# Moving five weight casts, one weight combination and five DRAM additions of x inside a fused attention, mixer and MLP kernel

## The chip, the core and the metric

The kernel runs on one core of a Trainium2 chip. The metric is the device time of one execution in microseconds (us), lower being better. TensorE (PE) does the matmuls and its separate weight loads (PEld), ScalarE (ACT) copies, casts and gelus, VectorE (DVE) additions and the attention arithmetic, GpSimd (POOL) a few small operations and all DMAs that add to their destination, and SyncE (SP) issues the plain DMAs.

## The reference, cut to what matters

With x of 2048 tokens by 576 channels and LN a layer norm without weights:

```python
xn = LN(x)
attn = sliding_window(xn @ wqkv, 32 heads of 18, 8 keys two tokens apart) @ wo
h    = shift_tokens(gelu(LN(xn) @ w1))          # by +1, -1, +2, -2 in four channel quarters
x1   = xn + h @ w2
mlp  = gelu(LN(x1) @ w3) @ w4                   # hidden size 4608
out  = x + attn + (x1 + mlp)
```

All data are float32. Each product is taken with both operands split into a float32r part and a rest, so that three (or, in the part below, seven) matmuls with chunks of the inner dimension stand where one would do.

## The kernel before, in words

The order of work on each engine is the order in which the program emits it, and the program is written out by hand. There are five stages: the qkv projection, the token mixer, four plain chunks of the MLP (the "units", 2 blocks of 128 hidden rows each), 28 groups of the MLP by a seven-product scheme, and the output projection of the attention with the final sums.

**The groups.** The scheme treats a pair of 128-row weight blocks and a pair of 512-token blocks as a 2x2 product and gets it with seven smaller products instead of eight, each of seven matmuls of 512 columns (function product, L1120 to L1133, matmul in L1130). They are called P1 to P7. Weights of group q lie in a tile WA[q] (w3a in the profile: A11, A22, A12) and a tile WS[q] (w3s: S1 to S4, sums and differences of blocks). The right-hand operands lie in five areas (x1n and xt in the profile). The loop over q (L1195) runs 28 times; q 0 to 13 (NWP = 14) work on tokens 0 to 1023, that is token tiles 0 to 7, and q 14 to 27 on tiles 8 to 15.

Between the products stand D0 to D7, the second MLP product of the group before it: each is one token tile (down, L859 to L881), 12 matmuls of 288 columns (L868), into one of two PSUM buffers. D0 to D3 take the tiles s0+4 to s0+7 and read the hidden halves c12 and c22, D4 to D7 the tiles s0 to s0+3 and read c11 and c21. After a tile's matmuls ACT empties the PSUM buffer, and then the buffer after next can be begun, seeded by ACT with the tile's running sum if that lies in SBUF. For the ten tiles in YD = (1, 2, 3, 5, 7, 9, 10, 11, 13, 15) the running sum lies in DRAM instead: ACT copies the PSUM buffer to one of a few staging tiles (L873) and POOL issues a DMA that adds it to yd[t] in DRAM (L874).

The order of a group is a string of item names; group 0 has an order of its own, in which only four tiles D0 to D3 stand, those of the last plain unit:

```python
ORDER = "P1 D0 P2 P6 D1 P5 D2 P7 D3 P4 D4 P3 D5 D6 D7"
ORDERS = {0: "P1 P2 D0 P6 P5 P7 D1 D2 P4 D3 P3", ...}
```

Products collect in PSUM, and ACT and DVE put them together: after P2 the first gelu (c11), after P6 and P7 a copy of the running bank by ACT ("keep", L1136), which the next product into that bank must wait for, and after P7 and P3 an addition by DVE (z_add, L1140). The addition behind P3 is the last one of the group; the gelus of c12 (L820, L821) follow it, and then low_part (L826), which takes the rest of the split. D0 of the next group is the first to read c12 and c22.

**The plan.** Everything else is hung on these items by at(item, function, arguments): it is emitted right behind the item, in the order of the at calls. What matters here:

- The next group's weights. load_pair (SP, L954 and L957) loads raw w3 blocks into the single tile w3st; split_a casts three blocks to WA (ACT L970 and L972, DVE L976) and lets POOL add a remainder from DRAM to its tail (L983); combine (L960 to L966) forms four sums and differences in w3st in place on DVE (L965, four instructions); split_s casts the result to WS and lets POOL add the tail (L992). In group 0 combine stood behind P4, ahead of D3 and P3, and low_part of c12 between the two halves of split_s.
- The output weight. In the last group (z = -1) five loads of wo rows go into tiles wr (SP, L1166 and L206) at the top of the loop body, and five split_wo follow (ACT cast L200, DVE subtraction L201), hung on D1, P5, D2, P7 and D4. Wo is first read by the output projection (L215), behind the last group's own eight D tiles.
- The residual x. load_xa(t) (L884 to L890) for a tile in YD lets POOL add x's tile to yd[t] by a DMA from DRAM to DRAM (L886). It was hung on D7 of groups 1 to 10, one tile of YD after the other.
- sums (L898 to L907): partial sums of the second half's operands, in DRAM, on D6 of groups 1 to 8; every other one is an adding DMA on POOL (L907).
- Attention runs on DVE in between: bg (L781) emits a few of its instructions behind every item until it is done.

**The end.** Behind the loop the last group's eight D tiles run back to back, with split_x of the attention's output blocks (ACT L181, L182, L187; DVE L183, L188) in between, then 16 token tiles of the output projection, 28 matmuls each (L215; the last tile L1437), with three PSUM buffers. DVE adds each to Y (L1431), for which load_y (SP, L1392) has brought the YD tiles back from DRAM. read_xo (SP, L174) loads the attention's output blocks; block 2 is loaded behind load_y of tiles 1, 2, 3 and 5.

Of the kernel before, what the change touches and what calls it, by code (L numbers as in the profile page):

```python
# [33 lines left out]
YD = (1, 2, 3, 5, 7, 9, 10, 11, 13, 15)  # L34
# [3 lines left out]
NWP = NF // 2 - NPL  # L38
# [19 lines left out]
def fused_block(ctx, tc, x, wqkv, wo, w1, w2, w3, w4, out):  # L58
# [448 lines left out]
    for b in range(NB):  # L507
        for i, m in enumerate((0, 1, 2, 4, 3) if b < 3 else (4, 0, 1, 2, 3)):
# [12 lines left out]
            k = {(0, 4): 0, (1, 1): 1, (1, 4): 2, (2, 1): 3, (2, 4): 4}.get((b, i))  # L521
# [102 lines left out]
    for t in range(NT):  # L624
# [19 lines left out]
        if t in (4, 5):  # L644
            r0, c0, n = ((256, 128, 128), (HF + 256, 0, 256))[t - 4]
# [8 lines left out]
        if t in (9, 10, 13, 14):  # L654
            k = {9: 4, 10: 6, 13: 8, 14: 10}[t]
# [168 lines left out]
    def low_part(h, g):  # L824
        spent[0] += 0.69
        dve.tensor_tensor(h[:, 1, :], g, h[:, 0, :].bitcast(F32), op=ALU.subtract)  # L826
# [182 lines left out]
    for u, (c, b) in enumerate(units):  # L1009
# [77 lines left out]
        k = u % 4  # L1087
# [107 lines left out]
    for q in range(NQ):  # L1195
        sb = q // NWP
# [28 lines left out]
        low12 = lambda: low_part(hid[q, "c12"], Z2)  # L1225
        n = q + 1
        plan = {}

        def at(it, f, *args):
            plan.setdefault(it, []).append(lambda: f(*args))  # L1230

        if q == 0:
            at("P6", split_op, 0, "T4")
            at("D1", gelu22)
            at("P7", split_a, n, (0, 1))
            at("D1", split_op, 0, "B22")
            at("D1", split_a, n, (2,))
            at("D2", low22)
            at("P4", combine, n)
            at("P3", gelu12)  # L1240
            at("P3", split_s, n, (0, 1))
            at("P3", low12)
            at("P3", split_s, n, (2,))
            at("P3", load_pair, q + 2)
        elif q == NWP - 1:
            rtemps[:] = [2, 13]
            at("P1", load_w4, p, 1)
            for it, k in zip(("P1", "P2", "P6", "P5", "P7", "P4", "P3"),
                             ("B11", "B21", "T2", "T1", "T3", "T4", "B22")):
                at(it, get_op, 1, k)  # L1250
            at("P4", split_w4, p)
            at("P3", split_op, 1, "B11", 0)
            at("D2", split_op, 1, "B11", 1)
            at("D3", gelu22)
            at("D4", low22)
            at("D4", split_op, 1, "B21", 0)
            at("D5", gelu12)
            at("D5", split_op, 1, "B21", 1)
            at("D6", low12)
            at("D6", split_op, 1, "T2", 0)  # L1260
            at("D7", split_op, 1, "T2", 1)
        elif q == NWP:
            rtemps[:] = [2]
            at("D0", split_op, 1, "T1", 0)
            at("D1", split_op, 1, "T1", 1)
            at("P1", split_op, 1, "T3", 0)
            at("D2", split_op, 1, "T3", 1)
            at("P2", split_op, 1, "T4", 0)
            at("P6", split_op, 1, "T4", 1)
            at("D3", split_op, 1, "B22", 0)  # L1270
            at("P5", split_op, 1, "B22", 1)
            at("P5", split_a, n, (0, 1))
            at("P7", split_a, n, (2,))
            at("P7", combine, n)
            at("D4", gelu22)
            at("P4", low22)
            at("D5", gelu12)
            at("D5", split_s, n, (0, 1))
            at("D6", low12)
            at("D6", split_s, n, (2,))  # L1280
            at("D7", load_pair, q + 2)
        elif z < -1:
            at("P1", load_w4, p, 1)
            at("P5" if q < NWP else "D2", split_a, n, (0, 1))
            at("D2" if q < NWP else "P7", split_a, n, (2,))
            at("D3", combine, n)
            at("P4", gelu22)
            at("D4", split_w4, p, 0)
            at("D4", low22)
            at("D5", split_w4, p, 1)  # L1290
            at("P3", split_s, n, (0, 1))
            at("D5", gelu12)
            at("D5", split_s, n, (2,))
            at("D6", low12)
            if z < -2:
                at("D6", load_pair, q + 2 + (q == NWP - 2))
        else:
            at("D3", split_w4, p)
            at("P4", gelu22)
            at("D4", low22)  # L1300
            at("D5", gelu12)
            at("D6", low12)
            for k, it in enumerate(("D1", "P5", "D2", "P7", "D4")):
                at(it, split_wo, k)
        if -5 <= z <= -2:
            for i, (it, nx) in enumerate((("P6", "D1"), ("P7", "D3"), ("P3", "D5"), ("D6", "D7"))):
# [6 lines left out]
            at("D5" if q else "P3", load_w4, NPL + pair(q + 1), 0)  # L1313
        if 0 < q < 9:
            at("D6", sums, 1, q - 1)
        if 0 < q <= len(YD):
            at("D7", load_xa, YD[q - 1])
        if -4 <= z < -1:
            at("P1", put_o, z + 4)
        if z == -2:  # L1320
# [149 lines left out]
```

## Time and profile before

| | before |
|---|---|
| median of three runs | 1298.65 us |
| lowest and highest | 1294.39, 1298.89 us |
| the profiled execution | 1297.69 us |
| its span in the trace | 1295.9 us |
| granted clock, mean | 0.993 |
| PE, DVE, ACT, POOL busy | 97%, 71%, 57%, 20% |
| DMA | 226.83 MB, mean 175 GB/s |

The span starts with the first instruction and ends with the last; the execution's own time is 1.79 us longer, for what lies around it. All times in the trace count from the span's start. A row of the timeline has the start, the duration, the engine (SPq is SP's sequencer, which issues DMAs), the line of the kernel, the operation and its tiles, and, in brackets, how long the engine had been idle before it and whose end released it. Rows merge neighbouring instructions of one kind (x7, x12). Matmuls are pipelined: from start to start, seven matmuls of a product take less than the duration of their row.

### The profile page before, as it was taken

What the parts mean: (1) busy time and instruction counts of PE and PEld (TensorE: products, weight loads), DVE (VectorE), ACT (ScalarE), POOL (GpSimd) and SP (SyncE); (2) the same over time, 40 slices, a digit from 0 to 9 for tenths busy, and PEclk for the clock granted to TensorE, in tenths of its full rate; (3) what the DMA queues carried; (4) which work ended last, traced back from release to release, by engine and by line L of the source; (5) the groups of instructions that cost most, each with busy time, mean ns of one, the idle gap of its engine ahead of it and who ended that gap; (6) DMA issues with size and microseconds to landing.
All of it is one profiled execution on the core that took longest, in us unless ns stands there. A gap on an engine that the chain in (4) does not pass through costs nothing. (4 is left out here: it accounts for less than half of the span.)

```text
span 1295.9 us, 20029 instructions
## 1 busy us (share of the span) xinstructions
PE 1262.2 (97%) x7482; PEld 1155.0 (89%) x7482; DVE 919.7 (71%) x1233; ACT 741.2 (57%) x1181; POOL 258.9 (20%) x374
## 2 busy tenths in 40 slices
PE   9999999999999999899999999998999999999798
PEld 8999998899899998799889988987899899899798
DVE  6456534778458978579989998988999983554342
ACT  3322226526545546677667776856876776776630
POOL 2011100021121212123222332211222222222100
PEclk9999999999999999999999999999999999999899
DMA  7646874256888987588888898696787769899872
GB/s 210 157 112 143 171 169 144 72 164 172 209 215 196 213 182 195 103 198 169 207 197 183 214 184 207 115 276 132 153 176 169 129 121 189 174 215 228 209 248 83
DMA packets 205565, 226.83 MB, mean 175 GB/s; under 512 B 79884, under 2 KB 140652, under 8 KB 205340
## 3 DMA queue, kind: packets, MB, share of 16 engines
q1 hardware_dynamic: 172332, 158.29, 43.0%
q0 software_dynamic: 33136, 67.26, 32.5%
q8 instruction: 59, 0.97, 0.3%
q14 instruction: 38, 0.31, 0.1%
HBM read 127.78 MB, written 107.97 MB: 182 GB/s over the span
## 5 line engine op out<-in xcount | busy, mean ns | idle before, releaser
L868 PEld LDWEIGHTS ps<-w,c 128*128 128x128 f32 x3456 | 480.0, 189 | 31.3 <-DVE Y L879 5.4
L868 PE MATMUL ps<-w,c 128*128 128x288 f32 x3456 | 492.6, 296 | 12.8 <-DVE Y L879 3.9
L874 POOL DMA_DIRECT2D yd<-Y x154 | 141.1, 919 | 365.9 <-ACT Y L873 315.3
L826 DVE TENSOR_TENSOR c<-Y,c 128x512 fp32r<-128x512 f32 x144 | 98.6, 686 | 85.3 <-ACT Y L815 80.3
L1130 PE MATMUL cc<-xt,w3s 128*128 128x512 f32 (+1 forms) x588 | 149.3, 393 | 1.8 <-DVE Y L1140 1.8
L873 ACT COPY Y<-ps 128x576 f32<-128x576 f32 x154 | 97.7, 635 | 71.0 <-PE ps L868 51.7
L215 PE MATMUL ps<-WQ,xt 128*128 128x432 f32 x672 | 134.8, 360 | 0.0
L215 PEld LDWEIGHTS ps<-WQ,xt 128*128 128x128 f32 x672 | 125.6, 188 | 5.7
L1130 PEld LDWEIGHTS cc<-xt,w3s 128*128 128x128 f32 (+1 forms) x588 | 107.5, 188 | 23.0 <-DVE Y L1140 2.2
L1130 PE MATMUL cc<-x1n,w3a 128*128 128x512 f32 x392 | 102.1, 399 | 2.7 <-DMA w3a<-w3t 2.7
L876 ACT COPY Y<-ps 128x576 f32<-128x576 f32 x92 | 58.8, 639 | 68.7 <-PE ps L868 67.2
L1130 PEld LDWEIGHTS cc<-x1n,w3a 128*128 128x128 f32 x392 | 71.7, 191 | 16.8 <-DMA w3a<-w3t 3.1
L746 DVE TENSOR_TENSOR po<-q,k 128x1152 f32<-128x1152 f32 (+1 forms) x48 | 84.2, 1755 | 0.8
L749 DVE TENSOR_REDUCE L<-po 128x64 f32<-128x1152 f32 (+1 forms) x48 | 84.0, 1751 | 0.8
L122 POOL TENSOR_TENSOR rs<-rs,mhalf 128x1 f32<-128x1 f32 x48 | 30.9, 643 | 258.3 <-DVE rs L121 147.7
L324 ACT COPY stg<-ps 128x864 f32<-128x864 f32 x24 | 21.2, 881 | 102.7 <-PE ps L215 55.8
L722 DVE TENSOR_TENSOR po<-v,L 128x1152 f32<-128x1152 f32 x56 | 75.7, 1354 | 0.9
L1140 DVE TENSOR_TENSOR Y<-cc,Y 128x512 f32<-128x512 f32 x57 | 39.1, 687 | 51.2 <-ACT Y L1136 48.3
L726 DVE TENSOR_TENSOR po<-po 128x1152 f32<-128x1152 f32 x49 | 66.4, 1354 | 0.8
L1130 PE MATMUL cc<-xt,w3a 128*128 128x512 f32 (+1 forms) x196 | 52.9, 410 | 9.9 <-ACT Y L1136 9.9
L965 DVE TENSOR_TENSOR w3st<-w3st 128x384 f32<-128x384 f32 x108 | 60.0, 556 | 3.1
L849 ACT COPY ps<-Y 128x576 f32<-128x576 f32 x92 | 59.3, 645 | 4.8 <-DVE Y L879 2.4
(192 smaller groups left out, 1898.6 us busy)
## 6 DMA issues: line engine op xcount, KB each, us to landing
yd<-Y POOLq DMA_DIRECT2D x156, 288.0 KB, 6.0
Y<-in_B_w_dram SPq DMA_DIRECT2D x31, 576.0 KB, 5.7
w3st<-in_B_w_dram SPq DMA_DIRECT2D x60, 256.0 KB, 8.0
qkvd<-stg SPq DMA_DIRECT2D x24, 432.0 KB, 3.8
yd<-ev POOLq DMA_DIRECT2D x26, 288.0 KB, 6.6
w3st<-in_B_w_dram SPq DMA_DIRECT2D x108, 64.0 KB, 8.0
xd<-st SPq DMA_DIRECT2D x16, 320.0 KB, 6.0
xd<-big SPq DMA_DIRECT2D x16, 320.0 KB, 7.1
```

Source lines behind the costliest of these rows:

```text
L215: pe.matmul(ps[:, h, :n], xs(a), ws(b, h), start=i == 0, stop=i == len(PAIRS) - 1)
L722: dve.tensor_tensor(dst, vv, Lf[:, :, w:w + 1].to_broadcast([128, TPP * GH, HD]), op=ALU.mult)
L726: dve.tensor_tensor(o, o, dst, op=ALU.add)
L746: dve.tensor_tensor(dst, qf[:, None, :].to_broadcast([128, n, TPP * GC]), win, op=ALU.mult)
L749: dve.tensor_reduce(Lw[:, w:w + n, :], dst.rearrange("p w (x d) -> p w x d", d=HD), axis=AX.X, op=ALU.add)
L826: dve.tensor_tensor(h[:, 1, :], g, h[:, 0, :].bitcast(F32), op=ALU.subtract)
L849: act.copy(ps[:, :, :HF], halves(t))
L868: pe.matmul(ps[:, k, :HF], h[:, col], w[:, p, k * HF:(k + 1) * HF], start=n == 0 and not seed, stop=n == len(seq) - 1, skip_group_check=True)
L873: act.copy(e.rearrange("p (h c) -> p h c", h=2), ps[:, :, :HF])
L874: pool.dma_start(yd[t], e, accum_op=ALU.add)
L965: dve.tensor_tensor(st[:, :, o, :], st[:, :, o, :], st[:, :, i, :], op=op)
L1130: pe.matmul(ps, WX[w][:k, v, SLOT[w], :], area[sb][xk][:k, a, :], start=onto is None and i == 0, stop=last and i == len(HALVES) - 1, skip_ ...
```

## The change

Three moves; nothing is added or taken away.

1. In group 0 combine for group 1 goes from P4 to P3, behind the last addition and the gelus of c12; low_part of c12 now stands behind combine and ahead of split_s.
2. In the last group the five split_wo go from D1, P5, D2, P7, D4 to P4, D4, P3, D5, D6. Their loads stay.
3. load_xa for the YD tiles, once behind D7 of groups 1 to 10, now goes behind D7 of groups 1 to 5 for tiles 9, 10, 11, 13, 15 and of groups 15 to 19 for tiles 1, 2, 3, 5, 7: always a tile of the half that the groups are not working on.

```diff
@@ group 0
             at("D2", low22)
-            at("P4", combine, n)
             at("P3", gelu12)
+            at("P3", combine, n)
+            at("P3", low12)
             at("P3", split_s, n, (0, 1))
-            at("P3", low12)
             at("P3", split_s, n, (2,))
             at("P3", load_pair, q + 2)
@@ last group
             at("D6", low12)
-            for k, it in enumerate(("D1", "P5", "D2", "P7", "D4")):
+            for k, it in enumerate(("P4", "D4", "P3", "D5", "D6")):
                 at(it, split_wo, k)
@@ every group
-        if 0 < q <= len(YD):
-            at("D7", load_xa, YD[q - 1])
+        if 0 < q - sb * NWP <= 5:
+            at("D7", load_xa, YD[5 - 5 * sb + q - sb * NWP - 1])
```

Here sb is 0 for groups 0 to 13 and 1 for groups 14 to 27. The lines are L1239 to L1242, L1303 and L1316 to L1317.

## The prediction

> **What bounds the kernel now.** The page first, then the list of PE's waits.
>
> ```profile
> span 1295.9 us, 20029 instructions
> ...
> PE 1262.2 (97%) x7482; PEld 1155.0 (89%) x7482; DVE 919.7 (71%) x1233; ACT 741.2 (57%) x1181; POOL 258.9 (20%) x374
> ```
>
> ```profile
> PE cc L1130 <- ACT Y L1136: 9.9, 5, 5.9
> ...
> PE cc L1130 <- DMA w3a<-w3t: 2.7, 1, 2.7
> ```
>
> PE is the bound: it is idle for 1295.9 - 1262.2 = 33.7 us. So an edit is worth the PE waits that it ends, and the slow matmuls that follow them, and nothing else. I took those waits one by one in the timeline. Three of the dearest stand exactly where the three edits are: 3.1 us at 540 (ACT and DVE behind combine), 2.71 at 667 (a weight tail added by POOL), 5.92 at 1207 (ACT behind the loads of wo). For a measure of undisturbed work, the chain that ended last gives a D tile and a product in a run without waits:
>
> ```profile
> 674.59 1.59 PE ps L868 x12
> 676.18 1.62 PE cc L1130 x7
> ```
>
> **First edit: combine behind the last addition.** The timeline where group 1 begins, some rows of it:
>
> ```profile
> 535.49 2.07 PE L1130 MATMUL cc<-x1n,w3a 128*128 128x512 f32 x7
> ...
> 537.01 2.33 DVE L965 TENSOR_TENSOR w3st<-w3st 128x384 f32<-128x384 f32 x4
> ...
> 539.26 0.68 DVE L1140 TENSOR_TENSOR Y<-cc,Y 128x512 f32<-128x512 f32 x1
> ...
> 540.66 0.80 PE L868 MATMUL ps<-w,c 128*128 128x288 f32 x4 [3.10 <-ACT c L820]
> ...
> 541.30 0.69 DVE L826 TENSOR_TENSOR c<-Y,c 128x512 fp32r<-128x512 f32 x1 [1.36 <-ACT Y L821]
> ...
> 542.05 2.14 PE L868 MATMUL ps<-w,c 128*128 128x288 f32 x8 [0.59 <-DVE c L826]
> ...
> 543.13 0.78 POOL L992 DMA_DIRECT2D w3s<-w3st  x1 [4.10 <-ACT w3s L972]
> ...
> 543.99 2.56 PE L1130 MATMUL cc<-x1n,w3a 128*128 128x512 f32 x7
> ...
> 546.39 1.77 PE L1130 MATMUL cc<-xt,w3s 128*128 128x512 f32 x7
> ```
>
> PE has ended P3 by 535.49, but the addition of its result waits on DVE until 539.26, behind the four instructions of combine (2.33 us). The gelu and D0 follow at once. Moved, the order on DVE is addition (537.0 to 537.7), combine (2.33, to 540.1), low_part (0.69, to 540.8); ACT runs the two gelus meanwhile, the first in some 0.7 us. D0's first four matmuls start at 538.4 instead of 540.66; its other eight need low_part and start at 540.85 instead of 542.05. That is **1.2 us**, not the whole 2.25, because combine now stands ahead of low_part: what is late next is low_part.
>
> A second part comes from the clock. D0's last eight matmuls took 543.99 - 542.05 = 1.94 us, where eight twelfths of 1.59 are 1.06, and P2 took 546.39 - 543.99 = 2.40 against 1.62: 1.66 us lost to a lower granted clock after 3.10 + 0.59 us of waiting. With waits of about 0.85 and 1.1 I expect none of it, because a wait of 2.31 elsewhere left the next tile quick:
>
> ```profile
> 867.09 1.85 PE L868 MATMUL ps<-w,c 128*128 128x288 f32 x12 [2.31 <-ACT Y L873]
> ```
>
> Its price: split_s and the tail's DMA now follow combine on ACT and POOL. They leave for POOL at about 542.1 (543.13 before). This DMA landed in:
>
> ```profile
> DMA to landing us min/median/max: 2.5/2.5/2.5
> ```
>
> so at 544.6, with P6's last matmul, which reads the tail, due at about 541.9 + 1.62 + 1.39 = 544.9. That fits barely; if the tail is a microsecond late, that one is lost. Bounds 0.2 to 2.9; I take **2.9**.
>
> The Trainium skill ("TensorE: Matmul & The Clock Gate", Part 1, what is actually happening) has the clock halved after an idle window of about 3.4 us. By that rule the waits of 2.71 below would not have cost any clock; the rows there show that one did, so the measurement decides.
>
> **Second edit: the casts of wo.** SP loads wr, ACT casts, PE stands:
>
> ```profile
> 1196.29 3.69 SPq L1166 DMA_DIRECT2D wr<-in_A_wo_dram  x4
> ...
> 1199.99 1.75 PE L868 MATMUL ps<-w,c 128*128 128x288 f32 x12
> ...
> 1201.72 0.67 ACT L200 CAST Wo<-wr 128x576 fp32r<-128x576 f32 x1 [5.72 <-DMA wr<-in_A_wo_dram]
> ...
> 1207.66 3.35 PE L1130 MATMUL cc<-xt,w3a 128*128 128x512 f32 x7 [5.92 <-ACT Y L1136]
> ...
> 1210.81 1.95 PE L868 MATMUL ps<-w,c 128*128 128x288 f32 x12
> ...
> 1225.18 8.20 PE L868 MATMUL ps<-w,c 128*128 128x288 f32 x60 [0.92 <-ACT Y L873]
> ...
> 1233.22 14.96 PE L215 MATMUL ps<-Wo,x1n 128*128 128x288 f32 x112
> ```
>
> The first cast stood behind D1 and held ACT for 5.72 us; the copy that P4 must wait for stood behind it. D3 was done at 1199.99 + 1.59 = 1201.58. From there to the output projection stand P4, D4, P3, D5 to D7 and eight more tiles: 2 x 1.62 + 12 x 1.59 = 22.3 us. They took 1233.22 - 1201.58 = 31.6: 9.3 too long, of it 6.1 the wait, 1.53 (3.15 for P4 against 1.62) and 0.21 (1.80 for D4 against 1.59) the clock, the rest short waits.
>
> Moved, ACT reaches the first cast at about 1204.9 and the fourth at 1210; the first tile had landed at 1201.72, 5.4 us after its issue, and the fourth, issued by 1200, should be there at 1206. So nothing waits for a load. But the same casts now stand among the drains of back-to-back tiles with two PSUM buffers. What ACT has to do in that stretch:
>
> ```profile
> core 0: us, PE busy (x) PEld busy (x) DVE busy (x) ACT busy (x) POOL busy (x), PEclk, DMA share, GB/s
> 1201.58:1233.22 31.64, 24.80 (x161) 23.12 (x159) 12.06 (x16) 22.06 (x36) 6.39 (x8) 0.89 0.87 218
> ```
>
> 22.06 us against PE's 22.3: ACT becomes nearly the bound. Laying its instructions out in order, ACT is 1.6 us behind at D7, and three tiles wait for a buffer, 0.9 + 0.7 + 1.3 = 2.9 us. So 9.3 - 2.9 = **6.4 us**; 7.8 if only the 1.5 of short waits stay that are there now (9.3 - 6.1 - 1.7), 4.4 if all five casts (5 x 0.67) add to those.
>
> The output projection must then be able to start earlier. Its first limit is the load of attention block 2, which SP issues behind load_y, and that waits for a staging tile to be added to DRAM:
>
> ```profile
> SPq L1392 <- DMA yd<-Y: 14.4, 1, 14.4
> ```
>
> ```profile
> 1241.60 0.62 ACT L181 CAST Y<-x1n 64x512 fp32r<-64x512 f32 x1 [5.41 <-DMA yd<-Y]
> ...
> 1244.99 0.75 DVE L1431 TENSOR_TENSOR Y<-ps,Y 128x576 f32<-128x576 f32 x1
> ...
> 1248.02 14.97 PE L215 MATMUL ps<-Wo,xt 128*128 128x288 f32 x112
> ```
>
> Tile 1's addition (done at 1245.74) stands on DVE behind block 2's split, and token tile 4 (1248.02) needs its buffer: 2.3 us of slack. The staging tile is that of D7, which comes forward with PE, so the load does too, and I count nothing.
>
> **Third edit: x where the tile is idle.** POOL's rows around the stop at 667, and two others:
>
> ```profile
> 655.91 0.84 POOL L886 DMA_DIRECT2D yd<-in_A_x_dram  x1 [8.25 <-issue]
> ...
> 660.62 0.88 POOL L874 DMA_DIRECT2D yd<-Y  x1 [3.87 <-ACT w3s L972]
> 661.16 1.14 POOL L983 DMA_DIRECT2D w3a<-w3t  x1
> ...
> 667.52 0.50 PE L1130 MATMUL cc<-x1n,w3a 96*128 96x512 f32 x1 [2.71 <-DMA w3a<-w3t]
> ```
>
> ```profile
> 664.80:674.59 9.79, 7.08 (x30) 5.93 (x30) 4.62 (x5) 5.67 (x10) 2.73 (x4) 0.83 1.04 225
> ```
>
> ```profile
> 805.07 1.88 PE L1130 MATMUL cc<-xt,w3a 128*128 128x512 f32 x7 [1.67 <-ACT Y L1136]
> ```
>
> At 655.91 POOL issues the addition of x to tile 5, and the next on POOL is D1's addition of group 5, to that same tile: it waits 3.87 us for x to land, and the weight tail (661.16) queues behind it, 6.3 us from landing. With tile 13 in tile 5's place, the wait of 3.87 goes; the tail is issued at about 657.4 and lands at 663.7, ahead of 664.8, where PE first stood. From 664.80 to 674.59 stand one matmul, a tile and two products, 0.23 + 1.59 + 3.23 = 5.05 us; it took 9.79, so **4.7 us** go. The 8.25 ahead of it (POOL behind the addition of a partial sum) stays; if that doesn't come forward with PE's 2.9 us, only 2.9 of the 4.7 are won.
>
> Five additions leave groups 6 to 10; the wait of 1.67 at 805 follows the last of them, when w3st came late. Five come into groups 15 to 19 and can make w3st late there. Bounds +1.9 to -3; I take nothing.
>
> **Sum:** 2.9 + 6.4 + 4.7 = 14.0 us from the profiled execution's 1297.69 (span 1295.9 and 1.8 around it): **1283.7 us**. The profiled execution lies 1 us under the median of the runs, 1298.65.
>
> **Rivals.**
> 1. POOL stays the bound at 667, behind the partial sum: +4.7, 1288.4. For it: the 8.25. Against: the 3.87 lies behind that.
> 2. The last stage hands its gain back: block 2's load does not come forward, and PE waits 6.4 - 2.3 = 4.1 us at token tile 4: 1287.8. Against: the staging tile that it waits for is itself moved forward.
> 3. The first edit does nothing, because the tail at P6 takes the place of the gelu at D0: +2.9, 1286.6.
> 4. Slower: in groups 16 to 20 the weights come late.
>
> ```profile
> 921.35 2.69 SPq L957 DMA_DIRECT2D w3st<-in_B_w_dram  x4
> ...
> 932.88 0.61 ACT L972 ACTIVATE w3a<-w3st,kv 96x384 fp32r<-96x384 f32 x1
> ```
>
> ```profile
> 934.01 1.45 PEld L1130 LDWEIGHTS cc<-xt,w3a 128*128 128x128 f32 x7 [0.24 <-ACT Y L1136]
> ```
>
> ```profile
> w3st<-in_B_w_dram SPq DMA_DIRECT2D x108, 64.0 KB, 8.0
> ```
>
> The last piece is issued by 923.6 and lands at about 931.6, ACT reads it at 932.88, and P4 already starts with the copy behind it: about 1.3 us of slack. Each addition of x that makes the load later by more than that stops PE in five groups one for one, from about 2.7 us of wait on with 1.7 of clock on top. To eat 14 us and 6.5 more it needs 4.1 per group, a load over 3.7 us late: 1304. The Trainium skill ("DMA: Bandwidth & Descriptors", Queues, rings and completion order) says that each DMA engine takes packets from its queues in turn, so an addition on POOL's queue slows SP's load beside it. Against it: with such additions in groups 7 to 11, PE stood 1.67 once. Half the price, 1290 to 1297, is likelier.
>
> **How the numbers follow.** Forecast 0.55 (1280 to 1288), rival 1 0.15, rival 2 0.10, rival 3 0.05, rival 4 in part 0.09, in full 0.06. A measurement here tells about 0.5%, 6.5 us, from no change, that is 1291.2. Below it lie the forecast, rival 3 and all but 0.05 of rivals 1 and 2 (where they meet): 0.80. Within: 0.05 + 0.09 = 0.14. Slower: 0.06. The range 1280 to 1292 leaves out rival 4 (0.15) and 0.05 below.
>
> **What would show it.** First edit: D0 of group 1 waits once for the gelu and once for low_part, about a microsecond each, P2 takes 1.6. Second: no ACT wait for wr, P4 directly behind D3, short waits at the last tiles, the output projection about 27 us after D3 of the last group begins (33.2 before). Third: no PE wait for w3a<-w3t. Wrong: a wait of more than a microsecond for L1136 in groups 16 to 20, or a PE wait in the output projection.

## The result, and the profile after

The kernel after takes 1283.28 us in the median of four runs (1279.72 to 1285.30), beside 1298.77 for the kernel before (four runs, 1294.39 to 1299.21). The ratio is 0.9885 with a 95% interval of 0.9854 to 0.9916: it is faster by 14.9 us, between 10.9 and 19.0. A second series of the same kernel gave 1283.41 and 0.9887 (0.9866 to 0.9907). The forecast was 1283.7. One execution of a kernel reported below, the one with the third edit alone, took 2057.42 us at a granted clock of 0.556; it is in none of the numbers.

The profiled execution took 1279.72 us, 18.0 less than the one of before. The page's first lines (busy time, share of the span, instructions) and rows from the list of PE's waits (us in total, times, longest):

```profile
span 1277.9 us, 20035 instructions
...
PE 1256.1 (98%) x7482; PEld 1149.9 (90%) x7482; DVE 919.6 (72%) x1233; ACT 742.3 (58%) x1181; POOL 259.4 (20%) x374
```

```profile
PE cc L1130 <- ACT Y L1136: 4.3, 4, 2.3
...
PE ps L868 <- DVE c L826: 1.4, 1, 1.4
...
PE ps L868 <- ACT c L820: 0.9, 1, 0.9
```

PE's idle time fell from 33.7 to 21.8 us (1277.9 - 1256.1), and its busy time by 6.1, since the same matmuls ran at a mean granted clock of 1.000 instead of 0.993 and fewer of them slowly. The wait for w3a<-w3t is gone, L1136 went from 9.9 to 4.3 us, L820 from 3.1 to 0.9; the 1.4 for low_part (L826) is new.

Not all of the 18.0 is the change's. The first row is of before, the second of after: the same D tile, in the plain chunks ahead of any edit, waits 2.77 us and runs slowly in one, 0.49 us and quickly in the other.

```profile
501.51 3.25 PE L868 MATMUL ps<-w,c 128*128 128x288 f32 x12 [2.77 <-DVE Y L879]
```

```profile
499.64 1.85 PE L868 MATMUL ps<-w,c 128*128 128x288 f32 x12 [0.49 <-DVE Y L879]
```

In the second series of after this wait was 1.94, so it differs from run to run. P1 of group 1 starts at 535.49 before and at 532.19 after, but at 535.24 in the second series: 3.3 of the 18.0 us lie ahead of the change and are chance.

**Group 1.** The timeline of after, the rows that answer to those of the first edit:

```profile
532.19 2.07 PE L1130 MATMUL cc<-x1n,w3a 128*128 128x512 f32 x7
...
533.73 0.69 DVE L1140 TENSOR_TENSOR Y<-cc,Y 128x512 f32<-128x512 f32 x1
...
534.34 2.33 DVE L965 TENSOR_TENSOR w3st<-w3st 128x384 f32<-128x384 f32 x4
...
535.14 0.80 PE L868 MATMUL ps<-w,c 128*128 128x288 f32 x4 [0.88 <-ACT c L820]
...
536.58 0.69 DVE L826 TENSOR_TENSOR c<-Y,c 128x512 fp32r<-128x512 f32 x1
...
537.32 1.32 PE L868 MATMUL ps<-w,c 128*128 128x288 f32 x8 [1.39 <-DVE c L826]
...
538.32 0.58 ACT L1333 COPY cc<-cc 128x512 f32<-128x512 f32 x1
...
538.72 0.78 POOL L992 DMA_DIRECT2D w3s<-w3st  x1 [2.97 <-PE ps L868]
...
538.95 1.87 PE L1130 MATMUL cc<-x1n,w3a 128*128 128x512 f32 x7 [0.31 <-ACT cc L1333]
...
540.66 1.77 PE L1130 MATMUL cc<-xt,w3s 128*128 128x512 f32 x7
```

The addition now stands ahead of combine, D0's first four matmuls wait 0.88 us instead of 3.10, and its other eight wait for low_part, which stands behind combine. With the 0.31 ahead of P2 the waits add up to 2.58 us, where before they were 3.10 + 0.59 = 3.69. P6 (540.66) does not wait for the tail.

**Group 5.** POOL's rows where PE stood at 667:

```profile
651.27 0.85 POOL L886 DMA_DIRECT2D yd<-in_A_x_dram  x1 [9.11 <-issue]
651.83 1.20 POOL L874 DMA_DIRECT2D yd<-Y  x1
652.38 1.46 POOL L983 DMA_DIRECT2D w3a<-w3t  x1
```

The wait behind the partial sum is still there (9.11, before 8.25), but the next addition goes to another tile and follows at once, and the weight tail with it: 8.8 us earlier than before, of which 4.6 are PE's lead when group 5 begins (its copy, L1333, starts at 636.38 instead of 641.02) and 4.1 are won within the group.

**The last group.** ACT's casts, PE's last waits and block 2 in the output projection:

```profile
1193.20 0.66 ACT L200 CAST Wo<-wr 128x576 fp32r<-128x576 f32 x1
...
1194.30 1.25 ACT L200 CAST Wo<-wr 128x576 fp32r<-128x576 f32 x2
...
1200.50 5.19 PE L868 MATMUL ps<-w,c 128*128 128x288 f32 x36 [0.53 <-ACT ps L849]
...
1206.52 0.64 ACT L873 COPY Y<-ps 128x576 f32<-128x576 f32 x1 [0.51 <-DMA yd<-Y]
...
1207.21 8.20 PE L868 MATMUL ps<-w,c 128*128 128x288 f32 x60 [1.53 <-ACT Y L873]
...
1215.25 14.96 PE L215 MATMUL ps<-Wo,x1n 128*128 128x288 f32 x112
...
1224.44 0.62 ACT L181 CAST Y<-x1n 64x512 fp32r<-64x512 f32 x1 [6.22 <-DMA yd<-Y]
...
1230.05 4.13 PE L215 MATMUL ps<-Wo,xt 128*128 128x288 f32 x30
```

No cast waits for wr. Two short waits are left, and the output projection starts 26.6 us after D3 (1188.62). Block 2's load came forward with PE, and token tile 4 (1230.05) does not wait.

### The profile page after: what moved, and what is told of

Read it like the earlier page. It is cut to its first block, busy times and chain, and to the rows that moved or that the text cites. A ratio compares the mean times of both kernels' runs of the same rounds, so it can differ in the third digit from the quotient of the medians.

```text
span 1277.9 us, 20035 instructions
## 1 busy us (share of the span) xinstructions
PE 1256.1 (98%) x7482; PEld 1149.9 (90%) x7482; DVE 919.6 (72%) x1233; ACT 742.3 (58%) x1181; POOL 259.4 (20%) x374
## 4 chain that ended last, share of the span: by engine, by line
PE 58%; DMA 5%; DVE 3%; issue 3%; ACT 2%; SPq 1%; POOL 0%; DVEq 0%; POOLq 0%; ACTq 0%
PE ps L868 27%; PE cc L1130 20%; PE p L832 6%; PE ps L215 4%; DMA w3st<-in_B_w_dram 3%; DMA x1n<-td1T 1%; DMA yd<-Y 1%; DMA xt<-td1T 1%; DVE w3st L965 1%; DVE c L826 0%; DVE po L722 0%; DMA xt<-td0T 0%; PE p L1437 0%; POOL yd L874 0%; SPq L957 0%
## 5 line engine op out<-in xcount | busy, mean ns | idle before, releaser
L826 DVE TENSOR_TENSOR c<-Y,c 128x512 fp32r<-128x512 f32 x144 | 98.7, 687 | 74.4 <-ACT Y L815 73.2
L873 ACT COPY Y<-ps 128x576 f32<-128x576 f32 x154 | 98.0, 637 | 63.8 <-PE ps L868 51.4
L1140 DVE TENSOR_TENSOR Y<-cc,Y 128x512 f32<-128x512 f32 x57 | 39.2, 687 | 57.2 <-ACT Y L1136 54.3
```

What stands on the lines that cost most here:

```text
L873: act.copy(e.rearrange("p (h c) -> p h c", h=2), ps[:, :, :HF])
```

## A ledger of stretches

Once per group ACT copies the bank of P1 (L1333). The time from one such copy to the next is a group's length whatever came ahead of it, and so kernels can be compared stretch by stretch. Undisturbed it is 24.06 us in groups 2 to 13 and 24.3 in 16 to 26. The columns: from the first matmul of P1 in group 1 to the copy of group 2; from copy to copy; and from the copy of group 27 to the first matmul of the output projection. All in us, from one profiled execution each.

| kernel | group 1 | 4 to 5 | 5 to 6 | 6 to 7 | 11 to 12 | last copy to projection |
|---|---|---|---|---|---|---|
| before | 31.94 | 25.47 | 28.70 | 24.15 | 26.02 | 44.28 |
| after | 29.52 | 26.55 | 24.06 | 24.34 | 24.06 | 37.68 |
| after, second series | 31.76 | 26.32 | 24.06 | 24.43 | 24.06 | 37.06 |
| combine alone | 29.54 | 25.34 | 28.90 | 24.98 | 24.90 | 44.14 |
| casts alone | 32.18 | 25.63 | 28.85 | 24.97 | 25.02 | 37.52 |
| x alone | 31.98 | 27.90 | 24.06 | 24.17 | 24.39 | 45.14 |
| before, tiles 5 and 7 swapped | 32.54 | 25.53 | 24.36 | 24.58 | 25.66 | 44.90 |
| after, x behind P4 | 29.51 | 26.73 | 24.06 | 24.06 | 24.51 | 37.05 |
| after, no x | 30.46 | 25.46 | 24.06 | 24.06 | 24.06 | 37.05 |
| after, low_part first | 34.29 | 26.81 | 24.06 | 24.62 | 24.06 | 37.06 |
| after, first cast at D1 | 30.47 | 28.00 | 24.06 | 24.06 | 24.06 | 43.72 |
| after, group 3 without x | 30.48 | 25.59 | 24.06 | 25.04 | 24.06 | 37.56 |

In the two profiles the change is worth 2.4 (group 1) + 6.6 (last stretch) + 4.6 (5 to 6) + 2.0 (11 to 12) - 1.1 (4 to 5) = 14.5 us. The differences of the other groups add up to 0.2; the largest are +2.1 at 13 to 14 and -1.0 at 14 to 15, which vary in all these kernels. With the 3.3 ahead of it that is the 18.0.

## The experiments

The theory is that of the forecast: three separate stops of PE, each ended by its own edit. The rivals are those of the forecast and, for each edit, that something other than what it names was the cause.

**Each edit alone.** The kernel before with one part of the diff:

```diff
-            at("P4", combine, n)
             at("P3", gelu12)
+            at("P3", combine, n)
+            at("P3", low12)
             at("P3", split_s, n, (0, 1))
-            at("P3", low12)
```

> The kernel before with the first edit alone. Theory: PE's two waits at D0 of group 1 shrink from 3.1 and 0.6 us to about 0.9 and 1.4 and the slow P2 behind them goes, so the stretch from P1 of group 1 to the first copy of group 2 shortens by 2.8 us, as it did between the two profiles (31.94 to 29.10); every later group is as long as before (26 us from group 11 to 12, 28.7 from group 5 to 6), and the whole is 2.8 us or 0.2% faster, about 1296. Rival: the weight tail of P6 takes the wait's place in a run where its DMA lands later than 2.5 us after its issue: the stretch shortens by under 1 us.

Measured: 1296.48 us, ratio 0.9985 (0.9969 to 1.0001), that is 1.9 us less, between -0.1 and 4.0. The profile shows the three waits of after again (0.88, 1.39, 0.30) and 29.54 us for the stretch, against 31.94 before and 29.52 in after (the 29.10 of the expectation is not what the profile of after has).

```diff
-            for k, it in enumerate(("D1", "P5", "D2", "P7", "D4")):
+            for k, it in enumerate(("P4", "D4", "P3", "D5", "D6")):
```

> The kernel before with the second edit alone. Theory: ACT no longer waits for wr in the last group; the stretch from the first copy of the last group to the output projection shortens by 6.6 us, as between the two profiles (44.3 to 37.7), and nothing else changes: about 1292 us. Rival: the gain in the two profiles came in part from the earlier start of everything ahead of it (11.4 us), which gave the loads of wr and of the attention blocks another place among the other transfers; then the stretch shortens by 4 us or less here.

Measured: 1290.80 us, ratio 0.9954 (0.9935 to 0.9973), 6.0 us less, between 3.5 and 8.4; the stretch at the end took 37.52 against 44.28.

```diff
-        if 0 < q <= len(YD):
-            at("D7", load_xa, YD[q - 1])
+        if 0 < q - sb * NWP <= 5:
+            at("D7", load_xa, YD[5 - 5 * sb + q - sb * NWP - 1])
```

> The kernel before with the third edit alone. Theory: the interval from group 5 to 6 falls from 28.7 to 24.1 us (no queue behind tile 5's x), the one from 11 to 12 from 26.0 to 24.1 (no x addition beside the load of w3st), the one from 4 to 5 grows by about 1 (the addition of x in group 3 starts sooner and meets the load of w3st), groups 16 to 20 stay at 24.3: 5.5 us in all, about 1293. Rival: POOL stands behind the partial sum's addition of group 4 in any case, and the queue at group 5 was broken up only because the first edit moved PE against it: then the interval from 5 to 6 stays above 27.

Measured: 1291.82 us in the median of six executions, ratio 0.9964 (0.9943 to 0.9985), by which it is 4.7 us less, between 1.9 and 7.4; 5 to 6 took 24.06 against 28.70, but 4 to 5 took 27.90.

The three add up to 12.6 us, inside the interval of the whole change. The time alone shows a gain for the second and the third edit; that of the first reaches to no gain at all, and rests on its stretch in the profiles. They do not need one another, and each stop is in every kernel that keeps its cause and in none that lacks it (the columns of group 1, 5 to 6 and the last).

**Is it the idle tile, or only another tile?** The kernel before with tiles 5 and 7 changed over in the order of x:

```diff
-            at("D7", load_xa, YD[q - 1])
+            at("D7", load_xa, (1, 2, 3, 7, 5, 9, 10, 11, 13, 15)[q - 1])
```

> The kernel before with x added to the same tiles in the same groups, only tiles 5 and 7 change places (7 in group 4, 5 in group 5), so that all of them are still busy tiles. Theory: the stop of PE at group 6's P1 comes from one meeting: x is added to tile 5 in group 4, late because of the partial sum ahead of it, and the very next addition on POOL goes to tile 5. With tile 7 there, the next addition goes to another tile, the weight tail behind it is issued 3.9 us sooner and the interval from group 5 to 6 falls from 28.7 to about 24.1. Rival: any x addition ahead of the tail slows it, whatever its tile, because the transfers share the DMA engines: 28 or more.

Measured: 1294.59 us in one run. POOL's rows in group 5:

```profile
655.61 0.85 POOL L886 DMA_DIRECT2D yd<-in_A_x_dram  x1 [8.84 <-issue]
656.17 1.19 POOL L874 DMA_DIRECT2D yd<-Y  x1
656.72 1.46 POOL L983 DMA_DIRECT2D w3a<-w3t  x1
```

The wait of 3.87 is gone and 5 to 6 takes 24.36 with x still added in the half that is being worked on. So the stop was a meeting of two additions to one tile, D1's behind x's, and changing two tiles' places ends it. Rival 1 (POOL stays the bound behind the partial sum) is out in this kernel and in after: the issue at L886 waits as long as before (in all three kernels it comes 0.3 us after the partial sum has landed), and PE does not stand.

**Does the place of combine matter, or only that the addition goes first?** The kernel after with low_part ahead of combine:

```diff
-            at("P3", combine, n)
             at("P3", low12)
+            at("P3", combine, n)
```

> The changed kernel with low_part of c12 ahead of combine in group 0. Theory: low_part is what is late at D0 of group 1 (PE's second wait, 1.39 us); ahead of combine it lets D0 go through, but combine, split_s and the weight tail come 1.3 us later, and P6 of group 1 then waits for them: the casts end at about 541, the tail lands at about 544, P6's last matmul would read it at 541, so P6 takes that wait over and the stretch from P1 of group 1 to the first copy of group 2 is 1 to 3 us longer than in the changed kernel (29.52), at 30.5 to 32.5. Rival: the tail had slack, and the stretch shortens by about 1.2 us, to 28.3.

Measured: 1285.75 us in one run, which lies among the runs of after, so only the stretch tells: it took 34.29, 4.8 more than in after, more than in before and more than the 30.5 to 32.5 that were expected.

```profile
537.30 2.33 DVE L965 TENSOR_TENSOR w3st<-w3st 128x384 f32<-128x384 f32 x4
537.43 2.19 PE L868 MATMUL ps<-w,c 128*128 128x288 f32 x8 [0.59 <-DVE c L826]
...
539.71 1.04 ACT L970 CAST w3s<-w3st 128x1024 fp32r<-128x1024 f32 x1 [3.05 <-DVE w3st L965]
...
541.28 0.57 ACT L1333 COPY cc<-cc 128x512 f32<-128x512 f32 x1
...
541.91 3.36 PE L1130 MATMUL cc<-x1n,w3a 128*128 128x512 f32 x7 [2.29 <-ACT cc L1333]
```

D0's wait for low_part fell to 0.59, as it should. But combine comes later, split_s waits 3.05 us for it on ACT, and behind split_s on ACT stands the copy that P2 must wait for. What took over was this copy, not the tail that P6 reads. In after the same queue costs the 0.31 us ahead of P2. But PE's waits alone (0.88 + 0.59 + 2.29 = 3.76 us, against 2.58 in after) make only 1.2 of the 4.8 us. The other 3.6 are slow matmuls: D0's last eight, P2 and P6 ran at a granted clock of 0.51 here and of 1.00 in after. With one profile, how much of that belongs to the order is not shown; the kernel with after's own order that was slowest there took 31.76.

**Is it the one cast that waits for its load?** The kernel after with the first of the five casts back at D1:

```diff
-            for k, it in enumerate(("P4", "D4", "P3", "D5", "D6")):
+            for k, it in enumerate(("D1", "D4", "P3", "D5", "D6")):
```

> The changed kernel with the first cast of wo back behind D1, the other four where the change put them. Theory: the stop in the last group was one wait, that of the first cast for its load; with it back, ACT waits 4 to 6 us again and the stretch from the last group's first copy to the output projection is 42 us or more (37.68 in the changed kernel, 44.28 before). Rival: the gain came from taking the casts as a whole out of ACT's dense stretch; then one cast costs a fifth of the 6.6 us, 39.

Measured: 1290.36 us in one run; the end takes 43.72 us.

```profile
1196.50 0.67 ACT L200 CAST Wo<-wr 128x576 fp32r<-128x576 f32 x1 [7.37 <-DMA wr<-in_A_wo_dram]
```

```profile
1198.96 3.35 PE L1130 MATMUL cc<-xt,w3a 128*128 128x512 f32 x7 [4.07 <-ACT Y L1136]
```

One early cast gives back 6.0 of the 6.6 us, so the places of the other four are worth 0.6 at most: it is the first instruction that waits, with P4's copy behind it on ACT.

**What do the additions of x still cost?** The kernel after with them behind P4 instead of D7, and without them:

```diff
-            at("D7", load_xa, YD[5 - 5 * sb + q - sb * NWP - 1])
+            at("P4", load_xa, YD[5 - 5 * sb + q - sb * NWP - 1])
```

> The changed kernel with x added behind P4 instead of D7, in the same groups and for the same tiles. Theory: the third edit's own cost, the interval from group 4 to 5 at 26.55 us against 25.47 before (ACT waits 4.1 us for w3st), comes from the addition of x in group 3 that runs beside that load; behind P4 it is some 7 us ahead of the load, the interval falls to 25.4 or less, and the whole is 1 to 2 us faster than the changed kernel, 1281.5 to 1282.5. Rival: the addition now stands ahead of the tail of w3s on POOL's queue, for which the load of w3st has to wait; the tail lands later, every group with an addition gets a wait for w3st, and the whole is 1 to 5 us slower than the changed kernel.

Measured: 1281.41 us, ratio 0.9882 (0.9853 to 0.9911).

```diff
-        if 0 < q - sb * NWP <= 5:
-            at("D7", load_xa, YD[5 - 5 * sb + q - sb * NWP - 1])
```

> The changed kernel without the additions of x to the ten tiles in DRAM: these ten tiles of the output lack x. Theory: what is left of their cost in the changed kernel is the wait at group 4, so the interval from group 4 to 5 falls from 26.55 to about 24.5 and no other moves by more than 0.4; the whole is 2 us faster, 1281. Rival: group 4 waits for w3st because the loads ahead of it (w4, the attention's, the addition of a partial sum) fill the DMA engines in any case, as before the change (25.47): then it stays above 25.3, and the ten additions cost nothing but their share of that.

Measured: 1282.33 us, ratio 0.9891 (0.9865 to 0.9916). Neither can be told from after: the ten additions cost nothing that a timing shows. Without x, 4 to 5 took 25.46 us, as the rival has it and not the 24.5 of the theory. Another stretch moved, which was not expected: 9 to 10 took 28.25 us against 24.67 in after, with a wait at P4 of group 9 and slow matmuls behind it.

```profile
747.61 2.33 PE L1130 MATMUL cc<-xt,w3a 128*128 128x512 f32 x7 [2.41 <-ACT Y L1136]
```

There the load of w3st is late (ACT waits 3.26 us for its first piece, 2.15 in after) in a kernel that adds no x at all. So what this profile wins at group 4 it loses at group 9, and the cause of the loss is not known. What x costs shows at group 4. P4 of group 4, in after, without x and with x behind P4, one row of each kernel:

```profile
624.88 1.87 PE L1130 MATMUL cc<-xt,w3a 128*128 128x512 f32 x7 [2.25 <-ACT Y L1136]
```

```profile
624.63 1.89 PE L1130 MATMUL cc<-xt,w3a 128*128 128x512 f32 x7 [1.12 <-ACT Y L1136]
```

```profile
626.46 1.87 PE L1130 MATMUL cc<-xt,w3a 128*128 128x512 f32 x7 [2.43 <-ACT Y L1136]
```

ACT's cast of w3st (L970) stands ahead of that copy and waits for the load. Without x PE's wait is 1.1 us, and in before 1.2, where POOL issued x only when tile 3's own addition had landed, 8.8 us after the group's copy (L1333) instead of 4.5 in after:

```profile
624.32 0.86 POOL L886 DMA_DIRECT2D yd<-in_A_x_dram  x1 [8.47 <-DMA yd<-Y]
```

The load itself shows the same. Counted from that copy, its last piece lands after 11.5 to 11.8 us in the six kernels in which x is issued some 9 us after the copy or not at all, and after 12.5 to 13.5 in the five profiles (after is there twice) in which x follows right behind the load, 4.4 to 5.0 us after the copy. So 1.1 of the 2.25 is x beside the load, and the rest is there without it. With x behind P4, x is issued at 601.59, lands at 607.97 and so is done before the load is issued (611.60), and the wait was there all the same, against what was expected: the last piece lands after 12.8 us. The transfers between the two are late in that kernel as well: counted from the copy, v (L699) lands after 2.1 us against 0.1 to 0.6 in the others, and Y (L562) after 8.6 against 6.5 to 6.9. So x may have held up the load by way of them; no run separates that.

**The same question by another way.** Group 3 without an x addition, group 6 with one, and after again beside it, six executions of each:

```diff
-        if 0 < q - sb * NWP <= 5:
-            at("D7", load_xa, YD[5 - 5 * sb + q - sb * NWP - 1])
+        if q in (1, 2, 4, 5, 6):
+            at("D7", load_xa, YD[5 + (1, 2, 4, 5, 6).index(q)])
+        if sb and 0 < q - NWP <= 5:
+            at("D7", load_xa, YD[q - NWP - 1])
```

> The kernel after, but in the first half the five x additions stand behind D7 of groups 1, 2, 4, 5, 6 instead of 1 to 5, so that group 3 has none. Theory: the addition of x that lands beside the load of w3st for group 5 makes that load late; in kernels where it was issued in that stretch (after, x alone, low_part first, first cast at D1) group 4 to group 5 took 26.55 to 28.00 us, in those where it came late or not at all (before, combine alone, casts alone, tiles swapped, no x) 25.34 to 25.63. So group 4 to 5 takes 25.3 to 25.7 us here, the wait at P4 in group 4 is about 1.1 us, nothing else moves, and the time is 1 to 2.5 us under that of the kernel after beside it. Rival: what is late there is the load itself and the partial sum that SP issues behind it, as the run with x behind P4 (26.73) suggests; then group 4 to 5 stays at 26.5 or more and the time stays. A second rival: the addition moved to group 6 makes a load late there, and group 6 to 7 or 7 to 8 takes what group 4 gave.

> The kernel after, unchanged, for the comparison on the same chip, and to see which of its waits come again. Theory: group 4 to 5 takes 26.5 to 28.0 us again, group 5 to 6 about 24.06, groups 16 to 20 about 24.3 each; the stretch from group 1's first product to group 2 takes 29.5 to 30.5; from the last copy of the loop to the output projection 37 to 38 us. Groups 13 to 15 vary by several us whatever the edit. Rival: group 4 comes out at 25.5 here, and then the wait of group 4 was no property of the kernel.

Measured: 1282.95 us, ratio 0.9880 (0.9862 to 0.9897), beside 1283.41, 0.9887 (0.9866 to 0.9907): no difference. After itself did not repeat in all: group 1 took 31.76 us where 29.5 to 30.5 was expected, and 4 to 5 took 26.32 where 26.5 or more was expected. PE's waits at P4 in groups 4 and 6 of the kernel without x in group 3, and the wait in group 4 of after's second series:

```profile
630.28 1.88 PE L1130 MATMUL cc<-xt,w3a 128*128 128x512 f32 x7 [1.28 <-ACT Y L1136]
...
679.36 1.89 PE L1130 MATMUL cc<-xt,w3a 128*128 128x512 f32 x7 [0.70 <-ACT Y L1136]
```

```profile
629.92 1.89 PE L1130 MATMUL cc<-xt,w3a 128*128 128x512 f32 x7 [2.00 <-ACT Y L1136]
```

Group 4 to 5 took 25.59 against 26.32, as the theory has it. Group 6 to 7 took 25.04 against 24.43, which has the size that the second rival wants but not its cause: by POOL's rows the addition that was moved was issued at 701.53 and lies in the stretch 7 to 8, which took 24.06, while group 6 has the same addition and loads beside it in both kernels. So these 0.6 us are a difference between runs, and they hide what group 4 gave. In all kernels but the one with x behind P4, group 4 to 5 takes 25.3 to 25.6 us where no x is issued right behind that load, and 26.3 to 28.0 where one is. No version here beats after by anything that can be measured.

## Why the prediction was right, point by point

**First edit, forecast 2.9, measured 2.4 in the two profiles, 1.9 (-0.1 to 4.0) in the timing.** The step "addition, combine, low_part" came as laid out: 0.88 for the gelu (forecast 0.85), then low_part, and PE's waits fell by 1.1 us (3.69 to 2.58) where the forecast has 1.2. The tail fits: it left POOL 6.5 us after P1's start (forecast 6.6), and P6 did not wait. Rival 3 is out. Two sizes were off. The wait for low_part was 1.39, not 1.1; the forecast's own rows give 540.85 - 538.4 - 0.80 = 1.65, so the 1.1 does not follow from them. And P2 waits 0.31 for ACT's copy, because split_s, now ready earlier, stands ahead of it; the forecast followed split_s to POOL and not to what stands behind it on ACT.

The part that hangs on the clock, 1.66 of the 2.9, failed as it was argued: "with waits of about 0.85 and 1.1 I expect none of" the lost clock, "because a wait of 2.31 elsewhere left the next tile quick". Seven profiles (after is there twice) have this order, all with waits of 0.87 or 0.88 and then 1.38 or 1.39, and in only three of them did D0 go on at full clock. The windows of 3.6 us that begin 0.2 us ahead of D0's second part, in after and in its second series (PE, PEld, DVE, ACT and POOL busy, then the granted clock):

```profile
537.09:540.69 3.60, 3.06 (x16) 2.54 (x17) 2.10 (x3) 3.57 (x7) 0.78 (x1) 1.00 0.55 84
```

```profile
540.20:543.80 3.60, 3.44 (x12) 3.16 (x13) 2.02 (x3) 3.57 (x7) 0.78 (x1) 0.50 0.53 80
```

and the rows of the second series:

```profile
540.36 2.29 PE L868 MATMUL ps<-w,c 128*128 128x288 f32 x8 [1.39 <-DVE c L826]
542.44 3.19 PE L1130 MATMUL cc<-x1n,w3a 128*128 128x512 f32 x7
545.43 2.29 PE L1130 MATMUL cc<-xt,w3s 128*128 128x512 f32 x7
```

The clock was 1.00 in one and 0.50 in the other after the same waits, and the stretch took 29.52 and 31.76. The four kernels with the old order took 31.94 to 32.54 (mean 32.2), the seven profiles with the new one 29.51 to 31.76 (mean 30.3): 1.9 us, the figure that combine alone gave in the timing. So a row of one profile cannot say that a wait of a given length is free of clock loss. The Trainium skill ("TensorE: Matmul & The Clock Gate", Part 1, what's actually happening) says that the gate looks at activity in a window that runs freely, so that the moment at which the clock changes depends on where in the window the work falls. That equal waits came out differently agrees with it; that a whole idle window of some 3.4 us is needed for the gate to close does not, for here the longest wait was 1.39.

**Second edit, forecast 6.4, measured 6.6 in the two profiles.** The count of undisturbed work (23.9 us from D3 on) and of what ACT's nearness would still cost (2.9) gave 26.8; the profile has 26.6, so 2.7 over. The forecast put it in three waits at the last tiles; it is two, 0.53 and 1.53, and some slowness. Part of the second is not ACT's work: ACT itself waited 0.51 for a staging tile (1206.52). In five other kernels with this order this second wait was 0.91 to 1.42 (0.92 in before, without the casts), and their last stretch took 37.05 to 37.56 us, 0.1 to 0.6 less than in after, so the 2.9 was somewhat too much. That block 2 comes forward with PE was right, and so rival 2 is out.

**Third edit, forecast 4.7, measured 4.6 at its place (5 to 6).** The wait of 3.87 was the cause and not the 8.25 ahead of it. The condition "if that doesn't come forward with PE's 2.9 us, only 2.9 of the 4.7 are won" did not arise: x was issued 4.6 us sooner (651.27, before 655.91). Everything else was taken as nothing between +1.9 and -3. It was two real things that nearly cancel: about 1 us lost at group 4, where x now lies beside the load, and 2.0 won at 11 to 12, where the wait of 1.67 at 805 went with the additions of groups 6 to 10 (in three other kernels that keep these additions the stretch took 24.90 to 25.66, so half of the 2.0 is this one profile's). Rival 4, the slower one, did not occur. Copies of groups 16 and 21 in after, ACT:

```profile
909.62 0.57 ACT L1333 COPY cc<-cc 128x512 f32<-128x512 f32 x1 [0.19 <-PE cc L1130]
```

```profile
1031.24 0.57 ACT L1333 COPY cc<-cc 128x512 f32<-128x512 f32 x1 [0.58 <-PE cc L1130]
```

The five groups 16 to 20 took (1031.24 - 909.62) / 5 = 24.32 us each, against 24.30 in before; the slack of 1.3 us was enough. The same addition beside the same load does cost in group 4, where SP also issues a partial sum (L905) right behind w3st. That alone does not make the difference: in after, group 2 has the same three transfers together (w3st from 562.24, x at 563.91, the partial sum at 565.55), and 2 to 3 took 24.06 us. What the traces show of group 4 alone is that PE waits 1.1 us for its load even without x, so there is no slack left to take up a later one; why that load is so late is not shown.

**The sum.** 14.0 forecast, 14.5 in the ledger, 14.9 (10.9 to 19.0) in the timing. It is right to a microsecond because the misses are of both signs: in the two profiles 0.5 too much for the first edit, 1.0 too little for the side effects of the third. The means of all profiles in the ledger with and without each edit say it more plainly: 1.9 for the first, 7.3 for the second, 4.4 for the third with its side effects (4.8 at 5 to 6, 1.3 at 11 to 12, -1.6 at 4 to 5), 13.6 in all. By these the first was 1.0 too high and the second 0.9 too low, and that they cancel is luck. That each edit ends the stop it names is shown by each edit alone.

**What stays open.** Groups 13 to 15, where the second half begins, take 29.5 to 33.5 and 24.0 to 25.8 us in these kernels, with waits for L873, L1136 and L1140 in changing places, whatever the edit.

## What to carry to other kernels

Where PE is 97% busy, price each of its waits in its own place and count the slow matmuls behind it: three moves of a few lines were worth 15 us though no engine did less work. Look for the instruction that waits at the head of an engine's queue and for what is behind it: one cast that ACT reached 7.4 us before its load had landed cost 6.0 of the 6.6 us of all five, and one DRAM addition to the tile that the next addition needs held a weight tail of another tensor. When something is moved, follow it on each engine's queue past what it feeds to what now stands behind it, and take a saving that hangs on the clock from several runs, not from one.

## What the hardware showed that was not expected

- The clock can fall to half after waits of 0.87 and 1.39 us with a short piece of work (0.80 us) between them, and in other runs stays full after the same waits. Longer single waits went both ways too: after 2.03, 2.13 and 2.41 us in three kernels the next seven or twelve matmuls were slow, after 2.25, 2.43 and 2.50 in three others they were quick.
- An addition to DRAM on POOL that must wait for an earlier one to the same tile holds all of POOL's later DMAs: 3.87 us at tile 5, 8.47 at tile 3. At tile 3 some 4 of the 8.47 are not of this kind, for in after, with another tile in its place, the same issue waits 4.21. The stop at tile 3 did good by chance: it kept x away from the load of the weights.
